# The opening of a linear-attention and gated-FFN kernel rearranged by head pairs, with two transfers and one set of transposes moved

## The chip, the cores and the metric

The kernel runs on one core of a Trainium2 chip. The metric is the device time of one execution in microseconds (us). Before the change the median of three runs is 323.31 us (322.63 to 324.01). The core has five engines with queues of their own: TensorE (PE; its weight loads are shown as PEld), VectorE (DVE), ScalarE (ACT), GpSimd (POOL) and SyncE (SP). SP and POOL also issue the transfers from and to memory.

## What is computed

Attention with cosine weights and without a softmax, on batch 8, 8 heads, 576 positions, head size 64, followed by a normalised gated feed-forward layer of width 1536:

```python
def phi(x, c, s):
    r = np.maximum(x, 0.0)
    return np.concatenate([r * c, r * s], axis=-1)     # c, s depend on the position
q_p, k_p = phi(q, cos_w, sin_w), phi(k, cos_w, sin_w)
kv  = np.einsum('bhsf,bhsd->bhfd', k_p, v)
z   = np.sum(k_p, axis=2)
num = np.einsum('bhsf,bhfd->bhsd', q_p, kv)
den = np.einsum('bhsf,bhf->bhs', q_p, z)[..., None] + 1e-06
x   = (num / den) as (4608, 512)                       # heads side by side
rms = np.sqrt(np.mean(x * x, axis=-1, keepdims=True) + 1e-06)
xn  = x / rms * rms_g
out = (silu(xn @ w_gate) * (xn @ w_val)) @ w_out
```

All inputs and the output are float32; the kernel multiplies in bfloat16.

## The kernel before, in words

The order of the work on each engine is the order of the calls in the source (`manual_schedule`, L49). An engine takes its instructions in that order. The order is written out by hand, and this is what the change edits.

**Blocks.** The rows of x are treated in blocks of 512 (four tiles of 128 rows, j = 0 to 3); block 0 is batch 0, and the last 64 positions of each batch are gathered in a block 8. For a block the steps n = 0 to 11 form gate and value for 128 columns of the hidden layer each (`half_mm`, L553, into psG and psV; silu on ScalarE; the product hT on VectorE), and the steps 12 to 15 form the output (`out_mm`, `out_store`). Work of the attention for the next batch is hung into these steps by the table `slots`: `at(block, step, where, function, ...)` enters it, `run` emits it. "pe" stands ahead of the step's products, "pre" ahead of its silu, "post" behind it.

**The attention of one batch.** `k_phi` makes kp (cosine part 0, sine part 1) from the raw k for one of nine chunks c, all four head pairs hp at once. `kvz_pe` multiplies kp by v (with a column of ones for z) into psA; `kvz_evac` copies the result to kvzs. `q_phi` and `q_tr_pe` make and transpose the q features of one tile, `q_tr_evac` copies them to qpT. `nd_pe` forms numerators and denominators of one tile in psA, `nd_post` takes the reciprocal and divides (VectorE) into xt, `x_sq` takes the mean square on ScalarE and the power on GpSimd, `x_norm` (VectorE) makes xn, `x_tr_pe` and `x_tr_evac` (or a transposing transfer) bring it to xnT.

**Batch 0** has functions of its own, since everything waits for it. z is summed by products with ones (`z0_pe`, a chunk at a time into zbank, copied to zrow by `z0_copy`, turned into columns by `z0_turn`); `kv0_pe` forms kv of one head pair from vv0, which a transfer casts on its way in; `kvz0_evac` copies both halves to kvzs. `nd0_pe` adds the 1e-6 by two small products (eps). q comes in two parts (`load_q0`), of two tiles each. `filler` issues products of zeros whose result is not read.

**Units.** The first eight steps of block 0 are cut into units (L631), so that they can begin with one tile of x: units 0 and 1 take one tile and four column blocks, units 2 and 3 two tiles and two column blocks, units 4 to 7 the other two tiles. `unit_mm` issues a unit's gate or value products, `unit_tile` those of one tile, `unit_silu` and `unit_h` the rest. L676 to L749 interleave the units with the tiles of batch 0, L913 to L923 go on with unit 5, the steps 8 to 10, `last_step` (step 11, into which the attention of batch 1 is hung) and `out_first` (the output of block 0, j-major, first the columns m of 0 to 7, then the rest; entries are run by the index of the product).

**Transfers.** SP issues k of batch 0, in two pieces by chunks, c 0 to 3 and c 4 to 8 (L149). POOL issues the rest of the opening in this order: q part 0, v in two transfers of two head pairs, q part 1, gate and value weights for n 0 to 3 and 4 to 7, k of batch 1, gate for n 8 to 11 (L211 to L229); then, among GpSimd's small operations, value for n 8 to 11, q and v of batch 1, the output weights wo in three transfers, k and v of batch 2. The raw tiles of k, q and v share a ring of five buffers.

Of the kernel before, what the change touches and what calls it, by code (L numbers as in the profile page):

```python
# [12 lines left out]
ALU = mybir.AluOpType  # L13
# [4 lines left out]
def kernel(  # L18
# [11 lines left out]
    nc = tc.nc  # L30
    B, H, S, D = q.shape
# [114 lines left out]

    g4 = one.tile([4, P], FP32, name="g4")
    nc.scalar.dma_start(out=g4[:, :], in_=moe_rms_g.rearrange("(t p) -> t p", p=P))
    for c0, c1 in ((0, 4), (4, NC)):  # L149
        nc.sync.dma_start(  # L150
            out=raw_kv("k", 0)[:, :, c0 * D : c1 * D],
            in_=kv_rows(k, 0, (0, HP))[:, :, c0 * D : c1 * D],
        )


    NTAB = 20
# [11 lines left out]
    masks.make_identity(nc, ident[:, :])  # L168
    mhalf = one.tile([P, 1], FP32, name="mhalf")
    G.memset(mhalf[:, :], -0.5)  # L170
# [3 lines left out]
    for i in range(NXT):  # L174
        G.memset(xts[i][:, DM : DM + 1], eps_col)


    wg = one.tile([P, NDT, DFF], BF16, name="wg")
# [30 lines left out]

    vv0 = one.tile([P, HP, NC * D], BF16, name="vv0")  # L210
    load_q0(0, G)  # L211
    for hp in range(0, HP, 2):
        G.dma_start(out=vv0[:, hp : hp + 2, :], in_=kv_rows(v, 0, (hp, hp + 2)))
    load_q0(1, G)
    for n in range(0, NNT - 4, 4):
        load_w(wg, moe_w_gate, n, n + 4)
        load_w(wv, moe_w_val, n, n + 4)

    eps_rows = one.tile([96, HP], BF16, name="eps_rows")
    eps_ones = one.tile([96, P], BF16, name="eps_ones")  # L220
# [5 lines left out]
        left -= part[i]  # L226
        G.memset(eps_rows[32 * i : 32 * i + 32, :], part[i] / 32)
    load_kv("k", 1, eng=G)
    load_w(wg, moe_w_gate, 8, NNT)  # L229

    def g_spread(bank, t):
        for i in range(3):
            nc.tensor.matmul(
                bank[:, t * P : (t + 1) * P], lhsT=sel[:, t, :], rhs=g3[:, i, :],
                start=(i == 0), stop=(i == 2),
            )
# [53 lines left out]
    def phi(eng, out_ap, in_ap, scale):  # L290
        if eng is A:
            A.activation(out=out_ap, in_=in_ap, func=AF.Relu, scale=scale)  # L292
# [114 lines left out]
    def z0_pe(c):  # L407
        for g in range(2):
            lo, hi = 64 * g, 64 * g + 64
            nc.tensor.matmul(  # L410
                zbank[g][:, :], lhsT=ones[lo:hi, :], rhs=kp[lo:hi, c, :, :],
                start=(c == 0), stop=(c == NC - 1),
            )

    def z0_copy(eng, g):
        copy(eng, zrow[:, g, :], zbank[g][0:1, :])
# [36 lines left out]


    def nd0_pe(j):
        for h in range(H):
            g, hp = h % 2, h // 2
            nc.tensor.matmul(
                heads[:, g, hp, :], lhsT=qpT[:, h, j * P : (j + 1) * P],
                rhs=kvzs[0][:, g, hp * E : (hp + 1) * E],  # L460
                start=(hp == 0), stop=False, skip_group_check=True,
            )
        for g in range(2):
            nc.tensor.matmul(
                heads[:, g, :, D], lhsT=eps_ones[:, :], rhs=eps_rows[:, :],
                start=False, stop=True, skip_group_check=True,
            )

    def nd_tails_pe(pair):
# [133 lines left out]
    qbank = [psV[0], psA[:, 0, :], psV[0], psV[1]]  # L603
    g_parts()
    filler(10, psC[1])
    for c in range(NC):
        k_phi(V, 0, c, 0)
        k_phi(A if c < 8 else V, 0, c, 1)
        z0_pe(c)
        if c < NDT:  # L610
            g_spread(psC[0], c)
    kv0_pe(0)
    kv0_pe(1)
    for j in range(2):
        q0_phi(V, j, 0)
        q0_phi(A, j, 1)
        q_tr_pe(0, j, qbank[j])
    z0_copy(V, 1)
# [54 lines left out]

    HALF = DM // 2  # L676
# [3 lines left out]
    q0_phi(V, 2, 0)  # L680
    q0_phi(G, 3, 0)
    q0_phi(A, 2, 1)
    q0_phi(A, 3, 1)
    filler(2, psC[1])
    nd_post(0, 0)
    q_tr_pe(0, 2, qbank[2])
    filler(1, psC[1])
    x_sq(0, 0)
    load_w(wv, moe_w_val, 8, NNT)
    nd0_pe(1)  # L690
    q0_tr_evac(V, 2, qbank[2])
    filler(2, psC[1])
    q_tr_pe(0, 3, qbank[3])
    nd_post(0, 1)
    filler(1, psC[1])
    nd0_pe(2)
    x_sq(0, 1)
    load_q(1, eng=G)
    load_kv("v", 1, eng=G)
# [7 lines left out]
    q0_tr_evac(A, 3, qbank[3])  # L707
    x_norm(0, 1)
    nd_post(0, 2)
    filler(1, psG[1])  # L710
    unit_mm(0, wg, by_rows=True)
    x_tr_pe(0, 1, psC[0])
    x_tr_evac(V, 0, 1, psC[0])
    unit_mm(0, wv)
    x_sq(0, 2)
    load_wo(0, 4)
    unit_silu(0)
    nd0_pe(3)
    nd_post(0, 3)
    x_norm(0, 2)  # L720
    unit_mm(1, wg)
    unit_mm(1, wv)
    x_sq(0, 3)
    load_wo(4, 8)
    load_wo(8, 12)
    unit_silu(1)
    x_norm(0, 3)
    unit_mm(2, wg)
    x_tr_pe(0, 2, psC[1])
    x_tr_evac(V, 0, 2, psC[1])  # L730
    unit_silu(2)
    unit_h(0)
    unit_mm(3, wg, part=(0, 6))
    x_tr_pe(0, 3, psC[0])
    x_tr_evac(A, 0, 3, psC[0])
    unit_mm(3, wg, part=(6, 8))
    unit_silu(3)
    unit_h(1)
    unit_tile(4, 2)
    unit_mm(2, wv)  # L740
    unit_h(2)
    unit_tile(4, 3)
    unit_silu(4)
    unit_mm(3, wv)
    unit_h(3)
    unit_mm(5, wg)
    unit_mm(4, wv)
    unit_silu(5)
    unit_h(4)  # L749

# [12 lines left out]
        at(0, 5 + c // 3, "post", k_phi, V, 1, c, 0)  # L763
        at(0, 5 + c // 3, "post", k_phi, A, 1, c, 1)
    for j in range(4):
        at(0, (8, 8, 9, 10)[j], "post", q_phi, V, 1, j, 0)
        at(0, (8, 9, 10, 10)[j], "post", q_phi, A, 1, j, 1)
        bank = (psC[0], psC[1], psV[0], psV[1])[j]
        if j < 2:
            at(0, 10 + j, "pe", q_tr_pe, 1, j, bank)  # L770
            at(0, 10 + j, "pre", q_tr_evac, V, 1, j, bank)
# [24 lines left out]
    def last_step():  # L796
        n = NNT - 1
        g, v = banks_of(0, n)
        run(0, n, "pe")
        half_mm(0, n, wg, g)  # L800
        kvz_pe(1)
        sg = four.tile([P, TB], FP32, name="sg", tag="sg")
        A.activation(out=sg[:, :], in_=g[:, 0:TB], func=AF.Silu)
        kvz_evac(A, 1)
        run(0, n, "pre")
# [8 lines left out]
    for j, i in ((1, 6), (2, 11), (3, 19)):  # L814
        at(0, 12, i, x_first, j)
        at(0, 12, i, x_last, j - 1)
    at(0, 12, 9, q_tr, 3, psV[0])
    at(0, 12, 21, x_norm, 1, 3)
    at(0, 12, 21, load_q, 2)
    at(0, 12, 43, x_tr, 3, psV[0])  # L820
    for nb in range(2, B):
        b = nb - 1
# [136 lines left out]
```

## Time and profile before

| | us |
|---|---|
| median of three runs (lowest, highest) | 323.31 (322.63, 324.01) |
| span of the profiled execution, first to last instruction | 321.1 |
| TensorE busy in the span | 313.6 |
| first weight product (L643) starts | 17.3 |
| gate of step 8 (L556) starts | 32.5 |
| output of block 0 (L574) starts | 42.3 |

The span is that of one execution; the runs are other executions, whose time also holds what lies around the span. Times within the span are counted from its start.

When the opening's transfers landed, each as its issue plus the time to landing that the view of transfers gives:

| transfer | issue | landed |
|---|---|---|
| k, second piece (SP) | 1.2 | 6.7 |
| q part 0 | 1.95 | 8.6 |
| v, pairs 0 and 1 | 3.0 | 9.8 |
| v, pairs 2 and 3 | 3.8 | 11.4 |
| q part 1 | 4.4 | 12.7 |
| gate, value for n 0 to 3 | 5.2, 5.9 | 15.1, 17.9 |
| gate, value for n 4 to 7 | 6.6, 7.4 | 20.4, 23.5 |
| k of batch 1 | 9.0 | 26.5 |
| gate, value for n 8 to 11 | 10.1, 16.0 | 28.9, 31.5 |
| q, v of batch 1 | 17.4, 18.4 | 34.4, 37.4 |
| wo, three transfers | 20.5, 22.3, 23.8 | 39.8, 42.3, 44.9 |

In the lists of groups and in the timeline a line names start, length, engine, source line, operation, what is written and read, shapes and count; in brackets stand the idle time of the engine ahead of it and what ended that. Operations of one engine overlap a little, so a row's length is somewhat more than the distance to the next.

### The profile page before, as it was taken

Reading aid. Unit: us, or ns where it says so; the run is one execution under the profiler, and the core shown is the slowest. Engines: PE = TensorE matmul, PEld = TensorE weight load, DVE = VectorE, ACT = ScalarE, POOL = GpSimd, SP = SyncE. Lnnn points to the kernel's source line nnn. Section 1 sums busy time; section 2 is a strip of 40 time slices with the busy share of each in tenths; the row PEclk is TensorE's granted clock in tenths of the full one; section 3 lists DMA queues with packets and bytes.
Section 4 is the critical chain, followed back from the end, with each engine's and each line's share of the span. In section 5 each row is a group of like instructions: output and inputs, shape, how many; then the busy total and the mean of one; then the engine's idle time right before and its main releaser. Section 6 shows DMA issues by size and latency. Waiting matters only on the chain.

```text
span 321.1 us, 6023 instructions
## 1 busy us (share of the span) xinstructions
PE 313.6 (98%) x2274; PEld 162.4 (51%) x2310; DVE 185.4 (58%) x382; ACT 165.8 (52%) x322; POOL 40.5 (13%) x79
## 2 busy tenths in 40 slices
PE   7999999999999999999999999999999999999996
PEld 2689564544454445444544445544544444444444
DVE  7976977668457773777457644781676034204410
ACT  5766756754574466554744575446543233223321
POOL 9771211002001100010001100100011000000000
PEclk9999999999999999999999999999999999999999
DMA  7999999788999999999799959995522500041002
GB/s 232 239 270 269 282 329 227 201 183 190 223 226 211 187 263 187 221 247 182 162 186 230 197 163 200 197 217 163 99 59 41 116 33 0 0 102 31 1 35 98
DMA packets 80092, 53.76 MB, mean 167 GB/s; under 512 B 52235, under 2 KB 74047, under 8 KB 80063
## 3 DMA queue, kind: packets, MB, share of 16 engines
q1 hardware_dynamic: 73110, 41.25, 62.1%
q0 software_dynamic: 6944, 12.13, 15.5%
q8 instruction: 18, 0.29, 0.4%
q14 instruction: 12, 0.09, 0.1%
q10 hardware_dynamic: 8, 0.00, 0.0%
HBM read 37.83 MB, written 9.44 MB: 147 GB/s over the span
## 4 chain that ended last, share of the span: by engine, by line
PE 94%; DMA 2%; DVE 1%; issue 1%; POOL 1%; ACT 0%; POOLq 0%; ACTq 0%
PE psC L574 27%; PE psV L556 27%; PE psG L556 26%; PE psV L643 2%; PE psA L449 2%; DMA vv<-in_v_dram 2%; PE psG L574 2%; PE psG L643 2%; PE psA L387 2%; PE psA L394 1%; PE psA L474 0%; PE psV L363 0%; PE psG L430 0%; PE psC L546 0%; POOL raw L135 0%
## 5 line engine op out<-in xcount | busy, mean ns | idle before, releaser
L571 DVE TENSOR_TENSOR hT<-psV,sg 128x512 bf16<-128x512 f32 x99 | 68.2, 689 | 96.5 <-PE psV L556 64.1
L556 PE MATMUL psV<-xnT,wv 128*128 128x512 bf16 x344 | 89.6, 379 | 0.7 <-issue 0.2
L570 ACT ACTIVATE sg<-psG 128x512 f32<-128x512 f32 x99 | 58.6, 592 | 60.8 <-PE psG L556 52.7
L556 PE MATMUL psG<-xnT,wg 128*128 128x512 bf16 x337 | 88.5, 379 | 0.7 <-issue 0.2
L574 PE MATMUL psC<-wo,hT 128*128 128x512 bf16 (+1 forms) x400 | 88.4, 376 | 0.4
L574 PEld LDWEIGHTS <-hT 128*128 128x128 bf16 x456 | 43.1, 98 | 47.7
L556 PEld LDWEIGHTS <-wv 128*128 128x128 bf16 x400 | 39.0, 98 | 46.8
L556 PEld LDWEIGHTS <-wg 128*128 128x128 bf16 x400 | 37.0, 98 | 39.9 <-DVE xnT L288 0.2
L520 POOL TENSOR_TENSOR rs<-ms,mhalf 128x1 f32<-128x1 f32 x36 | 20.5, 570 | 193.9 <-ACT scr L515 193.7
L286 ACT COPY osb<-psC 128x512 f32<-128x512 f32 x32 | 18.7, 585 | 49.9 <-PE psC L574 46.1
L515 ACT ACTIVATE scr<-xt 128x513 bf16<-128x513 f32 x36 | 22.8, 635 | 23.3 <-DVE xt L499 22.3
L527 DVE SCALAR_TENSOR_TENSOR xn<-xt,rs,gb 128x512 bf16<-128x512 f32 (+1 forms) x37 | 26.9, 730 | 9.9 <-POOL rs L520 9.9
L292 ACT ACTIVATE kp<-raw,tab 128x256 bf16<-128x256 f32 (+2 forms) x51 | 28.8, 607 | 2.4 <-DMA raw<-in_k_dram 2.4
L499 DVE TENSOR_TENSOR xt<-psA,rec 128x512 f32<-128x512 f32 x36 | 24.9, 691 | 1.2
L292 ACT ACTIVATE qp<-raw,tab 128x512 bf16<-128x512 f32 (+1 forms) x36 | 23.3, 666 | 1.2 <-DMA raw<-in_q_dram 1.1
L294 DVE TENSOR_SCALAR kp<-raw,tab 128x256 bf16<-128x256 f32 (+2 forms) x53 | 20.1, 428 | 0.5 <-DMA raw<-in_k_dram 0.5
L294 DVE TENSOR_SCALAR qp<-raw,tab 128x512 bf16<-128x512 f32 (+1 forms) x34 | 15.3, 463 | 4.7 <-DMA raw<-in_q_dram 4.7
L449 PEld LDWEIGHTS <-qpT 128*128 128x128 bf16 x224 | 10.6, 97 | 6.6
L556 PE MATMUL psV<-xnT_tail,wv 128*128 128x512 bf16 x48 | 12.3, 379 | 0.1
L556 PE MATMUL psG<-xnT_tail,wg 128*128 128x512 bf16 x46 | 12.0, 379 | 0.1
L288 DVE CAST vv<-raw 116x1280 bf16<-116x1280 f32 (+1 forms) x13 | 11.1, 857 | 1.3 <-DMA raw<-in_v_dram 1.3
L449 PE MATMUL psA<-kvzs,qpT 128*128 128x65 bf16 x224 | 11.4, 193 | 0.0
(102 smaller groups left out, 177.7 us busy)
## 6 DMA issues: line engine op xcount, KB each, us to landing
out_dram<-osb SPq DMA_DIRECT2D x27, 256.0 KB, 2.3
raw<-in_q_dram SPq DMA_DIRECT2D x6, 1024.0 KB, 9.1
raw<-in_k_dram SPq DMA_DIRECT2D x5, 1120.0 KB, 8.8
raw<-in_v_dram SPq DMA_DIRECT2D x5, 1120.0 KB, 9.4
raw<-in_k_dram POOLq DMA_DIRECT2D x2, 1152.0 KB, 19.2
raw<-in_v_dram POOLq DMA_DIRECT2D x2, 1152.0 KB, 15.7
out_dram<-osb SPq DMA_DIRECT2D x17, 128.0 KB, 2.6
wg<-in_moe_w_gate_dram POOLq DMA_DIRECT2D x3, 512.0 KB, 13.8
```

The costliest lines, as they stand in the source:

```text
L286: A.copy(out=o, in_=i)
L292: A.activation(out=out_ap, in_=in_ap, func=AF.Relu, scale=scale)
L294: eng.tensor_scalar(out=out_ap, in0=in_ap, scalar1=scale, scalar2=0.0, op0=ALU.mult, op1=ALU.max)
L449: nc.tensor.matmul(heads[:, g, hp, :], lhsT=qpT[:, h, j * P : (j + 1) * P], rhs=kvzs[b][:, g, hp * E : (hp + 1) * E], start=True, stop=True,)
L499: V.tensor_tensor(out=xt[:, 0:DM].rearrange("p (hp g d) -> p g hp d", g=2, d=D), in0=heads[:, :, :, 0:D], in1=rec[:, :, :].unsqueeze(3).to ...
L515: A.activation(out=scr[:, :], in_=xt[:, 0 : DM + 1], func=AF.Square, scale=1.0 / math.sqrt(DM), accum_out=ms[:, :],)
L520: G.tensor_tensor(out=rs[:, :], in0=ms[:, :], in1=mhalf[:, :], op=ALU.pow)
L527: V.scalar_tensor_tensor(out=xn_of[(b, j)][:, c], in0=x_of[(b, j)][:, c], scalar=rs_of[(b, j)][:, :], in1=gb[:, c], op0=ALU.mult, op1=ALU. ...
L556: nc.tensor.matmul(bank[:, cols[0] : cols[1]], lhsT=w[:, t, n * P : (n + 1) * P], rhs=x[:, t, cols[0] : cols[1]], start=(t == 0), stop=(t ...
L570: A.activation(out=sg[:, :], in_=g[:, 0:TB], func=AF.Silu)
L571: V.tensor_tensor(out=hT[:, n, :], in0=v[:, 0:TB], in1=sg[:, :], op=ALU.mult)
L574: nc.tensor.matmul(bank[:, 0 : cols[1] - cols[0]], lhsT=hT[:, n, j * P : (j + 1) * P], rhs=wo[:, n, cols[0] : cols[1]], start=(n == 0), st ...
```

## The change

It touches the opening, the interleaving of units and tiles, and the places of batch 1's attention in steps 7 to 12.

- k of batch 0 is loaded by head pairs, (0, 1) and (2, 3), all nine chunks in a row of 2304 bytes, in place of two pieces by chunks.
- phi of k goes by the same two halves: the cosine part on VectorE as one operation per head pair over all chunks (`k0_phi`, the table as a broadcast operand), the sine part by chunks of 128x128, five on ScalarE and four on VectorE for the lower pairs, nine on ScalarE for the upper. `z0_pe` goes by halves too.
- POOL: ident, mhalf and the small memsets go behind q part 0 or further; v of batch 0 comes as three pairs and one; q part 1 goes behind the weights for n 0 to 3; v of batch 1 goes ahead of the weights for n 8 to 11 and of q of batch 1.
- The first two tiles of q are transposed among the kv products; z's copies are both on ScalarE, the two copies of qpT on VectorE, gb on ScalarE.
- phi, transposes and copies of q's tiles 2 and 3, and nd of tile 2, go from ahead of the first unit to between the units. q's tile 3 is on VectorE in place of GpSimd. The eps products stand ahead of the others in `nd0_pe`. The units are ordered anew; unit 5's gate goes by tiles.
- Batch 1: the casts of v one to two steps earlier, `kvz_pe` at the head of step 10 in place of the middle of step 11, `q_phi` at steps 10 (tiles 0, 1) and 11 (tiles 2, 3, behind `x_sq`), all four transposes from step 11 on.

```diff
-    for c0, c1 in ((0, 4), (4, NC)):
-        nc.sync.dma_start(
-            out=raw_kv("k", 0)[:, :, c0 * D : c1 * D],
-            in_=kv_rows(k, 0, (0, HP))[:, :, c0 * D : c1 * D],
-        )
+    for hps in ((0, 2), (2, HP)):
+        load_kv("k", 0, hps)
...
     load_q0(0, G)
-    for hp in range(0, HP, 2):
-        G.dma_start(out=vv0[:, hp : hp + 2, :], in_=kv_rows(v, 0, (hp, hp + 2)))
+    masks.make_identity(nc, ident[:, :])
+    for hps in ((0, 3), (3, HP)):
+        G.dma_start(out=vv0[:, hps[0] : hps[1], :], in_=kv_rows(v, 0, hps))
+    load_w(wg, moe_w_gate, 0, 4)
+    load_w(wv, moe_w_val, 0, 4)
     load_q0(1, G)
-    for n in range(0, NNT - 4, 4):
-        load_w(wg, moe_w_gate, n, n + 4)
-        load_w(wv, moe_w_val, n, n + 4)
+    G.memset(mhalf[:, :], -0.5)
+    for i in range(NXT):
+        G.memset(xts[i][:, DM : DM + 1], eps_col)
+    load_w(wg, moe_w_gate, 4, 8)
+    load_w(wv, moe_w_val, 4, 8)
...
     load_kv("k", 1, eng=G)
-    load_w(wg, moe_w_gate, 8, NNT)
+    load_kv("v", 1, eng=G)
...
+    def k0_phi(c0, c1, part, hps):
+        o = slice(0, D) if part == 0 else slice(D, F)
+        f = NTAB if part == 0 else 0
+        for hp in range(*hps):
+            V.scalar_tensor_tensor(
+                out=kp[:, c0:c1, hp, o],
+                in0=raw_kv("k", 0)[:, hp, c0 * D : c1 * D].rearrange(
+                    "p (c d) -> p c d", d=D
+                ),
+                scalar=0.0,
+                in1=tab[:, f + c0 : f + c1].unsqueeze(2).to_broadcast([P, c1 - c0, D]),
+                op0=ALU.max, op1=ALU.mult,
+            )
...
-    for c in range(NC):
-        k_phi(V, 0, c, 0)
-        k_phi(A if c < 8 else V, 0, c, 1)
-        z0_pe(c)
+    for c in range(5):
+        k_phi(A, 0, c, 1, low)
+    k0_phi(0, NC, 0, low)
+    for c in range(5, NC):
+        k_phi(V, 0, c, 1, low)
+    for c in range(NC):
+        k_phi(A, 0, c, 1, high)
+    k0_phi(0, NC, 0, high)
+    for c in range(NC):
+        z0_pe(c, low)
         if c < NDT:
             g_spread(psC[0], c)
+    q0_phi(V, 0, 0)
+    q0_phi(A, 0, 1)
+    for c in range(NC):
+        z0_pe(c, high)
+    q_tr_pe(0, 0, qbank[0])
+    q0_phi(V, 1, 0)
+    q0_phi(A, 1, 1)
     kv0_pe(0)
-    kv0_pe(1)
...
+    q_tr_pe(0, 1, qbank[1])
     z0_copy(A, 0)
     q0_tr_evac(V, 0, qbank[0])
-    q0_tr_evac(A, 1, qbank[1])
-    V.tensor_copy(out=gb[:, :], in_=psC[0][:, :])
+    z0_copy(A, 1)
+    q0_tr_evac(V, 1, qbank[1])
+    kv0_pe(1)
+    kv0_pe(2)
     z0_turn()
-    kv0_pe(2)
     kv0_pe(3)
     kvz0_evac(A, 0)
     kvz0_evac(V, 1)
+    A.copy(out=gb[:, :], in_=psC[0][:, :])
```

The interleaving after the first norm, as it is now (from the first unit on):

```python
    unit_mm(0, wg, by_rows=True)
    x_tr_pe(0, 1, psC[0]); x_tr_evac(V, 0, 1, psC[0])
    unit_silu(0)
    unit_mm(0, wv)
    q0_phi(V, 2, 0); q0_phi(A, 2, 1)
    unit_mm(1, wg)
    q_tr_pe(0, 2, qbank[2]); q0_tr_evac(V, 2, qbank[2])
    q0_phi(A, 3, 1)
    unit_silu(1)
    q0_phi(V, 3, 0)
    unit_mm(1, wv)
    nd0_pe(2); nd_post(0, 2); x_sq(0, 2)
    load_wo(4, 8)
    q_tr_pe(0, 3, qbank[3]); q0_tr_evac(A, 3, qbank[3])
    unit_h(0)
    unit_mm(2, wg)
    nd0_pe(3); nd_post(0, 3); x_sq(0, 3)
    unit_silu(2)
    x_norm(0, 2)
    unit_mm(3, wg)
    unit_h(1)
    x_tr_pe(0, 2, psC[1]); x_tr_evac(V, 0, 2, psC[1])
    unit_silu(3)
    load_wo(8, 12)
    x_norm(0, 3)
    unit_mm(2, wv); unit_h(2)
    unit_tile(4, 2)
    unit_mm(3, wv)
    x_tr_pe(0, 3, psC[0]); x_tr_evac(A, 0, 3, psC[0])
    unit_h(3)
    unit_tile(5, 2)
    unit_tile(4, 3)
    unit_silu(4)
    unit_mm(4, wv)
    unit_tile(5, 3)
```

And batch 1:

```diff
     for j in range(4):
-        at(0, (8, 8, 9, 10)[j], "post", q_phi, V, 1, j, 0)
-        at(0, (8, 9, 10, 10)[j], "post", q_phi, A, 1, j, 1)
...
+        at(0, 10 + j // 2, "post" if j else "pre", q_phi, V, 1, j, 0)
+        at(0, 10 + j // 2, "post" if j else "pre", q_phi, A, 1, j, 1)
+    at(0, 7, "post", v_cast, G, 1, (0, 2))
     at(0, 8, "post", load_kv, "k", 2, (0, HP), G)
-    at(0, 9, "post", v_cast, G, 1, (0, 2))
-    at(0, 10, "pre", v_cast, V, 1, (2, 4))
+    at(0, 8, "post", v_cast, V, 1, (2, 4))
+    at(0, 10, "pe", kvz_pe, 1)
+    at(0, 10, "pre", kvz_evac, A, 1)
...
         half_mm(0, n, wg, g)
-        kvz_pe(1)
+        q_tr_pe(1, 0, psC[0])
+        q_tr_evac(V, 1, 0, psC[0])
...
         half_mm(0, n, wv, v)
+        q_tr(1, psC[1])
         nd_pe(1, 0)
-        q_tr(2, psV[0])
         nd_post(1, 0)
         V.tensor_tensor(out=hT[:, n, :], in0=v[:, 0:TB], in1=sg[:, :], op=ALU.mult)
         x_sq(1, 0)
         run(0, n, "post")
...
-    at(0, 12, 9, q_tr, 3, psV[0])
+    at(0, 12, 4, q_tr, 2, psV[0])
+    at(0, 12, 10, q_tr, 3, psV[0])
```

More of the change, by code (lines that the diff above doesn't have):

```diff
@@ L167 @@
     ident = one.tile([P, P], BF16, name="ident")
-    masks.make_identity(nc, ident[:, :])
     mhalf = one.tile([P, 1], FP32, name="mhalf")
-    G.memset(mhalf[:, :], -0.5)
     NXT = 4
@@ L173 @@
     eps_col = math.sqrt(DM * 1e-6)
-    for i in range(NXT):
-        G.memset(xts[i][:, DM : DM + 1], eps_col)
     wg = one.tile([P, NDT, DFF], BF16, name="wg")
@@ L405, with z0_pe @@
     heads0 = [b[:, 0 : HP * E].rearrange("p (hp e) -> p hp e", e=E) for b in psG]
-    def z0_pe(c):
+    def z0_pe(c, hps):
         for g in range(2):
@@ L410, in z0_pe @@
             nc.tensor.matmul(
-                zbank[g][:, :], lhsT=ones[lo:hi, :], rhs=kp[lo:hi, c, :, :],
+                zbank[g][:, hps[0] * F : hps[1] * F], lhsT=ones[lo:hi, :],
+                rhs=kp[lo:hi, c, hps[0] : hps[1], :],
                 start=(c == 0), stop=(c == NC - 1),
@@ L455, in nd0_pe @@
     def nd0_pe(j):
+        for g in range(2):
+            nc.tensor.matmul(
+                heads[:, g, :, D], lhsT=eps_ones[:, :], rhs=eps_rows[:, :],
+                start=True, stop=False, skip_group_check=True,
+            )
         for h in range(H):
@@ L460, in nd0_pe @@
                 rhs=kvzs[0][:, g, hp * E : (hp + 1) * E],
[L461 to L466, printed above, removed]
+                start=False, stop=(hp == HP - 1), skip_group_check=True,
             )
@@ L600, in filler @@
             )
-    qbank = [psV[0], psA[:, 0, :], psV[0], psV[1]]
+    qbank = [psV[0], psA[:, 0, :], psC[1], psC[0]]
+    low, high = (0, 2), (2, HP)
     g_parts()
     filler(10, psC[1])
+    for c in range(5):
[3 more added lines that the diff above has]
+        k_phi(V, 0, c, 1, low)
     for c in range(NC):
-        k_phi(V, 0, c, 0)
-        k_phi(A if c < 8 else V, 0, c, 1)
-        z0_pe(c)
+        k_phi(A, 0, c, 1, high)
+    k0_phi(0, NC, 0, high)
+    for c in range(NC):
+        z0_pe(c, low)
         if c < NDT:
             g_spread(psC[0], c)
-    kv0_pe(0)
-    kv0_pe(1)
[L614 to L618, printed above, removed]
+    q0_phi(V, 0, 0)
[5 more added lines that the diff above has]
+    q0_phi(A, 1, 1)
+    kv0_pe(0)
+    q_tr_pe(0, 1, qbank[1])
     z0_copy(A, 0)
     q0_tr_evac(V, 0, qbank[0])
-    q0_tr_evac(A, 1, qbank[1])
-    V.tensor_copy(out=gb[:, :], in_=psC[0][:, :])
+    z0_copy(A, 1)
+    q0_tr_evac(V, 1, qbank[1])
+    kv0_pe(1)
+    kv0_pe(2)
     z0_turn()
-    kv0_pe(2)
     kv0_pe(3)
@@ L677 @@
     lo, hi = (0, NDT // 2), (NDT // 2, NDT)
-    filler(2, psC[1])
+    load_w(wg, moe_w_gate, 8, NNT)
+    filler(1, psC[1])
     nd0_pe(0)
[L680 to L684, printed above, removed]
+    filler(4, psC[1])
     nd_post(0, 0)
-    q_tr_pe(0, 2, qbank[2])
-    filler(1, psC[1])
     x_sq(0, 0)
-    load_w(wv, moe_w_val, 8, NNT)
     nd0_pe(1)
-    q0_tr_evac(V, 2, qbank[2])
-    filler(2, psC[1])
-    q_tr_pe(0, 3, qbank[3])
+    filler(6, psC[1])
     nd_post(0, 1)
[L695 to L699, printed above, removed]
     x_norm(0, 0, (0, HALF))
     x_norm(0, 0, (HALF, DM))
+    x_sq(0, 1)
+    load_w(wv, moe_w_val, 8, NNT)
+    load_q(1, eng=G)
+    load_wo(0, 4)
     x_tr_pe(0, 0, psC[0], lo)
@@ L713 @@
     x_tr_evac(V, 0, 1, psC[0])
+    unit_silu(0)
     unit_mm(0, wv)
-    x_sq(0, 2)
-    load_wo(0, 4)
-    unit_silu(0)
+    q0_phi(V, 2, 0)
+    q0_phi(A, 2, 1)
+    unit_mm(1, wg)
+    q_tr_pe(0, 2, qbank[2])
+    q0_tr_evac(V, 2, qbank[2])
+    q0_phi(A, 3, 1)
+    unit_silu(1)
+    q0_phi(V, 3, 0)
+    unit_mm(1, wv)
+    nd0_pe(2)
+    nd_post(0, 2)
+    x_sq(0, 2)
+    load_wo(4, 8)
+    q_tr_pe(0, 3, qbank[3])
+    q0_tr_evac(A, 3, qbank[3])
+    unit_h(0)
+    unit_mm(2, wg)
     nd0_pe(3)
     nd_post(0, 3)
+    x_sq(0, 3)
+    unit_silu(2)
     x_norm(0, 2)
[L721 to L728, printed above, removed]
+    unit_mm(3, wg)
+    unit_h(1)
     x_tr_pe(0, 2, psC[1])
     x_tr_evac(V, 0, 2, psC[1])
-    unit_silu(2)
-    unit_h(0)
-    unit_mm(3, wg, part=(0, 6))
+    unit_silu(3)
+    load_wo(8, 12)
+    x_norm(0, 3)
+    unit_mm(2, wv)
+    unit_h(2)
+    unit_tile(4, 2)
+    unit_mm(3, wv)
     x_tr_pe(0, 3, psC[0])
     x_tr_evac(A, 0, 3, psC[0])
[L736 to L741, printed above, removed]
+    unit_h(3)
+    unit_tile(5, 2)
     unit_tile(4, 3)
     unit_silu(4)
-    unit_mm(3, wv)
-    unit_h(3)
-    unit_mm(5, wg)
     unit_mm(4, wv)
+    unit_tile(5, 3)
     unit_silu(5)
@@ L765 @@
     for j in range(4):
-        at(0, (8, 8, 9, 10)[j], "post", q_phi, V, 1, j, 0)
-        at(0, (8, 9, 10, 10)[j], "post", q_phi, A, 1, j, 1)
[L768 to L771, printed above, removed]
+        at(0, 10 + j // 2, "post" if j else "pre", q_phi, V, 1, j, 0)
+        at(0, 10 + j // 2, "post" if j else "pre", q_phi, A, 1, j, 1)
+    at(0, 7, "post", v_cast, G, 1, (0, 2))
     at(0, 8, "post", load_kv, "k", 2, (0, HP), G)
-    at(0, 9, "post", v_cast, G, 1, (0, 2))
-    at(0, 10, "pre", v_cast, V, 1, (2, 4))
+    at(0, 8, "post", v_cast, V, 1, (2, 4))
+    at(0, 10, "pe", kvz_pe, 1)
+    at(0, 10, "pre", kvz_evac, A, 1)
     at(0, 10, "post", load_kv, "v", 2, (0, HP), G)
@@ L800, in last_step @@
         half_mm(0, n, wg, g)
-        kvz_pe(1)
+        q_tr_pe(1, 0, psC[0])
+        q_tr_evac(V, 1, 0, psC[0])
         sg = four.tile([P, TB], FP32, name="sg", tag="sg")
         A.activation(out=sg[:, :], in_=g[:, 0:TB], func=AF.Silu)
-        kvz_evac(A, 1)
-        run(0, n, "pre")
         half_mm(0, n, wv, v)
+        q_tr(1, psC[1])
         nd_pe(1, 0)
-        q_tr(2, psV[0])
         nd_post(1, 0)
@@ L812, in last_step @@
         run(0, n, "post")
-    for j, i in ((1, 6), (2, 11), (3, 19)):
+    for j, i in ((1, 6), (2, 12), (3, 20)):
         at(0, 12, i, x_first, j)
         at(0, 12, i, x_last, j - 1)
-    at(0, 12, 9, q_tr, 3, psV[0])
-    at(0, 12, 21, x_norm, 1, 3)
-    at(0, 12, 21, load_q, 2)
+    at(0, 12, 4, q_tr, 2, psV[0])
+    at(0, 12, 10, q_tr, 3, psV[0])
+    at(0, 12, 22, x_norm, 1, 3)
+    at(0, 12, 22, load_q, 2)
     at(0, 12, 43, x_tr, 3, psV[0])
```

2 lines of the change are left out of this document (removed).

## The prediction

> **What bounds the kernel now.** I read the engine totals first, then busy time by stretch, then the chain that ended last, then the timeline of the opening and of the last step of block 0.
>
> ```profile
> PE 313.6 (98%) x2274; PEld 162.4 (51%) x2310; DVE 185.4 (58%) x382; ACT 165.8 (52%) x322; POOL 40.5 (13%) x79
> ```
> ```profile
> 15.00:17.30 2.30, 2.09 (x27) 1.37 (x26) 1.84 (x6) 1.47 (x6) 2.08 (x4) 1.00 1.24 204
> 17.30:22.00 4.70, 4.70 (x84) 4.52 (x83) 3.65 (x8) 3.12 (x7) 3.37 (x6) 1.00 1.23 229
> 22.00:27.00 5.00, 5.00 (x60) 4.63 (x58) 2.97 (x5) 2.45 (x5) 1.83 (x3) 1.00 1.14 305
> 27.00:32.00 5.00, 5.00 (x48) 4.48 (x46) 3.87 (x9) 3.74 (x9) 0.75 (x1) 1.00 1.15 288
> ```
> In the second fence each line is a stretch, its length, then busy time of PE, PEld, DVE, ACT, POOL, the granted clock, the DMA share and GB/s. From 17.3 us on TensorE has no gap. So there are two places to look: when the first weight product (L643) starts, and what is put between products afterwards. Whatever is inserted there, or makes TensorE wait there, adds one for one to the end.
>
> ```profile
> 3.02 6.81 DMA vv<-in_v_dram
> ...
> 12.56 0.43 DVE kvzs L288
> ...
> 17.46 0.90 PE psG L643 x16
> ...
> 19.60 0.24 PE psA L458 x8
> ...
> 36.08 0.45 PE psC L363 x8
> ```
> The chain (start, length, what): v's first half arrives at 9.83, the state of batch 0 is copied out (L288) at 12.56, the first product follows 4.9 us later. The last two pieces are prices: the eight products of one tile (numerator and denominator, "nd") hold TensorE 0.24 us, eight head transposes 0.45.
>
> ```profile
> 5.04 3.42 ACT L292 ACTIVATE kp<-raw,tab 128x256 bf16<-128x256 f32 x8 [2.38 <-DMA raw<-in_k_dram]
> ...
> 17.15 1.02 ACT L286 COPY qpT<-psV 128x1024 bf16<-128x1024 bf16 x1
> ...
> 19.44 0.41 PE L458 MATMUL psA<-kvzs,qpT 128*128 128x65 bf16 x8
> ...
> 19.91 0.21 DVE L487 RECIPROCAL rec<-psA 128x8 f32<-128x8 f32 x1 [0.49 <-PE psA L464]
> ...
> 20.16 0.69 DVE L499 TENSOR_TENSOR xt<-psA,rec 128x512 f32<-128x512 f32 x1
> ...
> 20.76 0.74 DVE L527 SCALAR_TENSOR_TENSOR xn<-xt,rs,gb 128x512 bf16<-128x512 f32 x1
> ...
> 20.96 0.64 ACT L515 ACTIVATE scr<-xt 128x513 bf16<-128x513 f32 x1 [0.54 <-DVE xt L499]
> ...
> 21.59 0.58 ACT L666 ACTIVATE sg<-psG 128x512 f32<-128x512 f32 x1
> ```
> This is one tile's path from its products to its norm. Products to reciprocal 0.47 (0.43 once the eps products stand first), 0.25 to the division, which holds VectorE 0.60 and ends after 0.69; 0.11 to the square; the square holds ScalarE 0.63; the copy of the transposed q on ScalarE takes 1.02.
>
> **Opening.** The same bytes are moved. v is issued about 0.2 earlier on POOL (four memsets and mhalf leave, ident now follows q's first part). k's two transfers came at 4.96 and 6.7 (issue 1.19 + 5.5) and I keep 5.0 and 6.7. ScalarE's phi of 128x128 is not in the trace: its 128x256 form repeats every 0.40 (three in 1.29, 0.50 each), the 128x512 form every 0.61 (two in 1.32), so between 0.20 and 0.40; the line through both gives 0.30. Five from 5.0, nine from 6.7: 9.4. Four q phi (1.70 in the trace): 11.1. Two zrow copies (0.56 each, 0.46 apart): 12.1. VectorE's 128x576 is nearest the norm of 128x512, which repeats every 0.67 (128x256: 0.40), so 0.74, between 0.67 and 0.85; four of them and four 128x128 (0.30; the 128x256 cost 0.26 to 0.50) end at 9.3. TensorE then sums z of the upper pairs (nine times 0.11): 10.3, transposes: 10.75, forms pair 0: 11.0, transposes after ScalarE: 11.6, forms pairs 1 and 2 (36 products in 0.54): 12.15. z's turn 0.28, pair 3 0.44 to its end: 12.85, where before the copy began at 12.54. nd gains 0.08, since VectorE's q phi no longer stands in front of its reciprocal. Net **+0.2**. Bounds: v is complete at 11.36 before (issue 3.76 + 7.6), 0.2 earlier now, so not under -1.2; at 0.40 per ScalarE phi, +1.6.
>
> **Work moved behind the first product.** Two tiles' q transposes and the nd of tile 2, which ran among filler products: 2 x 0.45 + 0.24 + 0.03 = **+1.17**. The fillers taken out stood ahead of the chain's last wait and give nothing. Units 4 and 5 have the same columns in another order: 0.
>
> **New waits among the units.** Engines take their work in program order; the changed order is printed by engine.
> (a) nd of tile 3 needs the copy of q's tile 3, which ScalarE now does behind the square of tile 2, and that needs nd of tile 2. From nd 2 on: 0.43 + 0.25 + 0.69 + 0.11 + 0.63 + 1.02 + 0.03 = 3.16. TensorE has nd 0.24, transposes 0.47, unit 2's gate 0.87, eps 0.05: 1.63. Wait **1.5** (1.2 to 1.7).
> (b) x's transposes of tile 2 need its norm, which VectorE does behind the division of tile 3: 0.43 + 0.25 + 0.60 + 0.75 + 0.03 = 2.06, against nd 0.24 and unit 3's gate 0.87. **0.95** (0.8 to 1.1).
> (c) The second tile of unit 4 reads x's tile 3, whose copy on ScalarE (0.58) follows its transposes (0.22, and 0.20 to the copy): 1.03 with 0.03, against 0.22 and one unit tile of 0.45. **0.36** (0.2 to 0.5). Before, 0.22 + 0.45 + 0.87 of products stood between.
>
> **Last step and output of block 0.** The phi of q's tiles 2 and 3 of batch 1 now goes out after the square of its tile 0; before it was done by 40.2. From nd_pe(1, 0): 1.80 to that square (41.64 to 43.44 in the timeline), 0.63 for it, 0.71 for ScalarE's phi, 0.03: 3.17. The transposes of tile 2 stand four output products later: 0.24 + 4 x 0.216 = 1.10. Wait **2.05** (1.7 to 2.2). Behind them on TensorE stand all later output products. The state of batch 1 goes to the start of step 10 with the same products; its copy on ScalarE (0.59) comes off the last step, where the chain shows 0.16 of issue: left at 0.
>
> **Queues.** POOL: a transfer there waits for an earlier one to land (wo: 0.71 behind wv at 23.80). q's second part goes behind the first two weight blocks, so it lands where the second of these did, 17.9 (5.90 + 12.0); ScalarE first wants it at 18.8 after unit 0's silu: nothing, and one for one beyond that. Gate and value of n 8 to 11 go behind v of batch 1 and land about 3.0 later (v took 34.4 to 37.4), at 31.9 and 34.4; they were read at 32.47 and 33.33 and now some 4.2 later, so the delay itself hides it. v of batch 1 lands by 30, and its casts, now two steps earlier, keep up. The powers of tiles 2 and 3 stand behind wo's issues, which wait for landings of 17.9 and 20.4; they are wanted at 23 and 26. SP keeps its two k transfers; q of batch 2 moves by one output product.
>
> **Sum.** 0.2 + 1.17 + 1.5 + 0.95 + 0.36 + 2.05 = 6.2. The profiled execution's span 321.1 becomes 327.3; it lies 2.2 under the median of the runs, 323.31, which becomes **329.5**. The bounds add up to +3.9 (-1.2 + 1.17 + 3.9) and +8.3 (1.6 + 1.17 + 5.5), so 327.2 to 331.6.
>
> **Rivals.**
> Overtaking: TensorE runs the next ready product past one that waits. Then the four waits (4.86) fill and only 0.2 + 1.17 stay: 324.7, no change. It decides if all but 0.2 us of the waits is filled. For it: a weight load of L430 was issued at 8.91, its product at 9.87. Against it: q's first transposes were ready at about 9.5 (both phi done) and stood behind products that waited for v until 9.87; they ran at 10.51, in order. 0.06. The Trainium skill ("TensorE: Matmul & The Clock Gate", Part 2, step by step) says that only weight loads are pulled ahead and products keep program order; by that rule this rival is out, and the trace agrees with 10.51 against 9.5.
> Clock: TensorE now idles from 5.0 to about 6.7 and near 8 to 9.3. If the granted clock halves, as in the first ten fillers (3.90 us for ten, 0.22 each later), about 1.7 us of products before 11.2 double, about 1.0 of it on the path: 330.5. Against it: the clock column reads 1.00 in all stretches, also over the gap of 0.57 before 9.87. 0.07. The same page, Part 1, halves the clock after an idle window of about 3.4 us; by it gaps of 1.7 and 1.3 cost nothing, and no run yet shows a gap so long here.
> Late q: its second part lands 1 us after 18.8; ScalarE holds unit 1's silu behind it: 330.5. Transfers run without a pause until 51 us, which speaks for some lateness. 0.06.
> v's arrival sets the opening (-1.2 instead of +0.2): 328.1, in the forecast's own range.
> That the change doesn't do what it says is ruled out by the printed order.
>
> **Chances.** Forecast with its bounds 0.72, overtaking 0.06, clock 0.07, late q 0.06; 0.09 for shorter waits than I priced together with an opening nearer v's arrival, half of it reaching no change, half faster. Measurement can't tell under 0.5% (1.6 us). Faster 0.05, same 0.10, slower 0.85. Range 327.2 to 331.6: it leaves out overtaking and most of the last case.
>
> **What would show it.** Right: first product near 17.5; TensorE waiting about 1.5 for a qpT copy, 0.9 for xn, 0.4 for an xnT copy between 22 and 31, and 2 us before the transposes of qp near 47; weights never waited for. Wrong: no such gaps, or a first product before 16, or a TensorE wait on a transfer.

## The result, and the profile after

The changed kernel takes 331.76 us (median of four runs: 332.96, 333.09, 329.58, 330.56) against 323.31: 2.5% slower, ratio 1.0254, 95% interval 1.0208 to 1.0301. The forecast was 329.5, and the median lies 0.16 above the end of its range, 331.6. The profiled execution is the one of 332.96; its span is 331.2, 10.1 above the 321.1 of before. Laid side by side at four marks, first start to first start:

| stretch (us) | before | after | difference | forecast |
|---|---|---|---|---|
| start to first weight product | 17.31 | 20.43 | +3.12 | +0.2 |
| from there to the gate of step 8 (units) | 15.16 | 20.18 | +5.02 | +3.98 |
| steps 8 to 11 | 9.86 | 9.42 | -0.44 | no price of its own; transposes of 0.45 cross the mark |
| output of block 0, to the first product of block 1 | 11.76 | 14.16 | +2.40 | +2.05, and those 0.45 |
| rest | 267.01 | 267.01 | 0 | 0 |

The engine totals of the changed kernel:

```profile
PE 319.1 (96%) x2303; PEld 165.0 (50%) x2339; DVE 185.8 (56%) x380; ACT 167.8 (51%) x330; POOL 37.2 (11%) x77
```

TensorE's busy time went from 313.6 to 319.1 and its idle time from 7.5 to 12.1. The busy time by stretch (start and end, length, then PE, PEld, DVE, ACT, POOL, clock, DMA share, GB/s) says where the idle time sits:

```profile
20.43:40.61 20.18, 17.17 (x225) 15.36 (x224) 14.48 (x28) 11.39 (x25) 7.77 (x11) 1.00 1.15 288
40.61:50.03 9.42, 9.31 (x129) 5.40 (x128) 5.69 (x11) 5.31 (x11) 0.00 (x0) 1.00 1.02 312
50.03:64.19 14.16, 12.27 (x96) 6.44 (x95) 10.26 (x24) 9.44 (x19) 2.20 (x4) 1.00 0.26 57
```

In the units TensorE is idle for 3.01 of 20.18 us, where before it had no gap at all; in the output of block 0 for 1.89 of 14.16 (before 0.05 of 11.76). No other engine is near its limit. The timeline (start, duration, engine, line, what; in brackets the idle time before it and what ended that) names the waits:

```profile
26.34 0.63 ACT L528 ACTIVATE scr<-xt 128x513 bf16<-128x513 f32 x1 [2.10 <-DVE xt L512]
...
26.97 0.99 ACT L284 COPY qpT<-psC 128x1024 bf16<-128x1024 bf16 x1
...
28.02 0.42 PE L476 MATMUL psA<-kvzs,qpT 128*128 128x65 bf16 x8 [1.28 <-ACT qpT L284]
...
30.13 0.40 PE L559 MATMUL psC<-ident,xn 128*128 128x128 bf16 x4 [0.81 <-DVE xn L540]
...
30.93 2.43 DVE L540 SCALAR_TENSOR_TENSOR xn<-xt,rs,gb 128x512 bf16<-128x512 f32 x1
...
31.64 1.16 POOL L286 CAST vv<-raw 128x1152 bf16<-128x1152 f32 x1
...
33.41 0.40 PE L559 MATMUL psC<-ident,xn 128*128 128x128 bf16 x4 [0.69 <-DVE xn L540]
...
34.48 0.61 PE L682 MATMUL psG<-xnT,wg 128*128 128x128 bf16 x8 [0.23 <-ACT xnT L284]
...
52.84 0.62 PE L375 MATMUL psV<-ident,qp 128*128 128x128 bf16 x8 [1.79 <-ACT qp L290]
```

Five waits of TensorE. Four are those of the forecast, on the releasers it named; the first two lines show the square of tile 2 on ScalarE (26.34) and behind it the copy (26.97) that the first wait is for. The wait at 33.41 was not forecast: the norm of tile 3 on VectorE took 2.43 us, over three times its usual 0.75, beside a cast of batch 1's v on GpSimd. A wait costs TensorE more than its idle figure, because products are pipelined and the modelled end of the last one before the gap reaches about 0.17 us past its turn. Counted from start to start, against the time the products ahead of it take in an unbroken row (0.87 for a unit's eight products of 256 columns), they cost 1.41, 0.98, 0.86, 0.39 and 1.95.

The opening is the larger surprise. In its timeline the first line is the ten fillers:

```profile
1.19 4.45 PE L611 MATMUL psC<-warm 128*128 128x512 bf16 x10 [1.19 <-DVE warm L161]
...
6.28 0.39 PE L422 MATMUL psC<-kp,ones 64*128 64x256 bf16 x1 [0.64 <-DVE kp L312]
...
11.63 0.42 PE L422 MATMUL psC<-kp,ones 64*128 64x256 bf16 x1
11.63 0.42 PE L422 MATMUL psV<-kp,ones 64*128 64x256 bf16 x1
11.84 0.42 PE L422 MATMUL psC<-kp,ones 64*128 64x256 bf16 x1
```

The pairs of z products stand 0.21 apart, twice the 0.11 that the forecast took, and still do so at 11.84. A filler of 512 columns takes 0.43, as the first seven of before do. TensorE ran at half its clock until about 13.6 us, where the first clock event of the trace stands; before, that event came at 4.4. The clock column of the views shows 1.00 ahead of the first event, so there the length of a known product has to be read instead.

### The profile page after: what moved, and what is told of

Same layout as the page of the kernel before. It is cut to its first block, busy times and chain, and to the rows that moved or that the text cites. A ratio compares the mean times of both kernels' runs of the same rounds, so it can differ in the third digit from the quotient of the medians.

```text
span 331.2 us, 6086 instructions
## 1 busy us (share of the span) xinstructions
PE 319.1 (96%) x2303; PEld 165.0 (50%) x2339; DVE 185.8 (56%) x380; ACT 167.8 (51%) x330; POOL 37.2 (11%) x77
## 4 chain that ended last, share of the span: by engine, by line
PE 92%; DVE 3%; ACT 2%; DMA 1%; issue 1%; POOL 0%; ACTq 0%
PE psC L587 26%; PE psV L569 26%; PE psG L569 26%; PE psA L462 2%; PE psA L399 2%; PE psG L587 2%; PE psV L667 1%; PE psC L422 1%; DMA raw<-in_k_dram 1%; PE psG L667 1%; DVE xn L540 1%; DVE xt L512 1%; PE psA L406 1%; ACT scr L528 1%; PE psV L375 1%
## 5 line engine op out<-in xcount | busy, mean ns | idle before, releaser
L540 DVE SCALAR_TENSOR_TENSOR xn<-xt,rs,gb 128x512 bf16<-128x512 f32 (+1 forms) x37 | 28.6, 776 | 9.0 <-POOL rs L533 9.0
L290 ACT ACTIVATE kp<-raw,tab 115x512 bf16<-115x512 f32 (+3 forms) x57 | 29.7, 569 | 2.2 <-DMA raw<-in_k_dram 2.2
L292 DVE TENSOR_SCALAR qp<-raw,tab 128x512 bf16<-128x512 f32 (+1 forms) x36 | 16.0, 460 | 4.7 <-DMA raw<-in_q_dram 4.7
L292 DVE TENSOR_SCALAR kp<-raw,tab 115x512 bf16<-115x512 f32 (+3 forms) x47 | 17.3, 415 | 0.0
```

Of the source, the lines that this page charges most:

```text
L292: eng.tensor_scalar(out=out_ap, in0=in_ap, scalar1=scale, scalar2=0.0, op0=ALU.mult, op1=ALU.max)
L540: V.scalar_tensor_tensor(out=xn_of[(b, j)][:, c], in0=x_of[(b, j)][:, c], scalar=rs_of[(b, j)][:, :], in1=gb[:, c], op0=ALU.mult, op1=ALU. ...
```

## The experiments

Each is an edit of one place, unless the text says otherwise. The ratio is to the kernel before, timed beside it on the same chip (323.25 or 323.03 there). The stretches are those of the table above, in the profiled execution.

**16 fillers in place of 10.**

```diff
-    filler(10, psC[1])
+    filler(16, psC[1])
```

> The changed kernel with 16 instead of 10 filler products in front of the sums of z. Theory: in the changed kernel's trace the full clock was granted only from 13.6 us (4.4 in the kernel before), so the products up to there took twice their time and the first weight product came at 20.4; six more filler products bring the full clock by 8.1 at the latest, the first weight product comes at 17.4 to 18.2 and the span shrinks by 2 to 3 us to about 328.5. Rival: phi of k and the copies on ScalarE and VectorE are slower than priced and set the opening; then the first product stays at 20 or later, and moves later by up to 1 us because the sums start behind the fillers.

Measured 330.21 us (329.49 to 331.44), ratio 1.022 [1.0191, 1.0248]; profiled span 327.7. TensorE in the opening of this run:

```profile
1.19 5.44 PE L611 MATMUL psC<-warm 128*128 128x512 bf16 x16 [1.19 <-DVE warm L161]
...
9.06 0.27 PE L422 MATMUL psC<-kp,ones 64*128 64x256 bf16 x1
9.06 0.27 PE L422 MATMUL psV<-kp,ones 64*128 64x256 bf16 x1
9.17 0.27 PE L422 MATMUL psC<-kp,ones 64*128 64x256 bf16 x1
...
10.14 0.62 PE L375 MATMUL psV<-ident,qp 128*128 128x128 bf16 x8
...
17.66 0.55 PE L667 MATMUL psG<-xnT,wg 128*128 128x128 bf16 x7
```

The z products stand 0.11 apart, the first transposes start at 10.14 (after: 12.41), and the first weight product at 17.66 instead of 20.43: 2.77 of the opening's 3.12 was the clock. What is left, 0.35, is the forecast's +0.2 within its bounds; up to 0.29 of it may be the fillers themselves, since the first z products came at 6.57 instead of 6.28. The full clock came at 4.91 here, when ten fillers would still have been running (all at half speed, they end at 5.64). So this execution does not show that six more bring it sooner; what they did was to fill the gap ahead of the z products, and the clock was not lost again.

The units took 19.32 instead of 20.18, though nothing in them was changed. The cast of v now stands 1 us behind the norm of tile 3, which takes 0.75 again:

```profile
28.16 0.75 DVE L540 SCALAR_TENSOR_TENSOR xn<-xt,rs,gb 128x512 bf16<-128x512 f32 x1
...
29.88 1.14 POOL L286 CAST vv<-raw 128x1152 bf16<-128x1152 f32 x1 [1.00 <-DMA raw<-in_v_dram]
```

**A late clock in the kernel before.** The same cause, put into the other kernel: five fillers in place of ten.

> The kernel before with 5 instead of 10 filler products at its start. Theory: the full clock then comes later than 4.4 us, the first weight product moves from 17.3 to between 18.5 and 20.5, and the whole run is 1 to 3 us longer: the price of a late clock by itself, without any other part of the change. Rival: the clock does not depend on those fillers, or the opening is set by v's arrival at 9.8 with enough room behind it: first product at 17.3 to 17.6, no change in time.

325.25 us (324.78 to 325.85), ratio 1.0066 [1.0041, 1.009]. The z products ran at half speed (0.42 apart, where a filler of as many columns takes 0.22 at full clock), the full clock came at 12.7, the first weight product at 19.53 instead of 17.31, and the rest of the kernel was unchanged. So a late clock alone costs this kernel 2.2 us in the profiled execution, 2.0 in the median.

**The cast of v on VectorE.**

```diff
-    at(0, 7, "post", v_cast, G, 1, (0, 2))
+    at(0, 7, "post", v_cast, V, 1, (0, 2))
```

> The changed kernel with both halves of batch 1's v cast on VectorE (steps 7 and 8); GpSimd casts nothing. Theory: the norm of tile 3 took 2.43 us instead of 0.75 since GpSimd's cast ran beside it (31.64 to 32.80); without it the norm takes 0.75 and the wait of 0.7 to 1.0 us in front of tile 3's transposes goes: minus 0.9 us between the first weight product and the gate of step 8 (20.2 us, 19.3 expected). Rival: the norm is slow for another reason (its power is late, or the transfer issues on GpSimd beside it); then it still takes 2 us or more and nothing is gained.

331.42 us (330.59 to 332.3), ratio 1.0254 [1.0221, 1.0286]. The norm of tile 3 in this run:

```profile
31.08 0.75 DVE L540 SCALAR_TENSOR_TENSOR xn<-xt,rs,gb 128x512 bf16<-128x512 f32 x1
```

It is back at 0.75, its wait is gone, the units took 19.32 (0.86 less), and steps 8 to 11 lost nothing by the cast (9.41). The runs hardly show it, since the opening, which was late here too (20.58), varies by more from run to run.

**The phi of q's tiles 2 and 3 of batch 1 at step 10.**

```diff
-        at(0, 10 + j // 2, "post" if j else "pre", q_phi, V, 1, j, 0)
-        at(0, 10 + j // 2, "post" if j else "pre", q_phi, A, 1, j, 1)
+        at(0, 10, "post" if j else "pre", q_phi, V, 1, j, 0)
+        at(0, 10, "post" if j else "pre", q_phi, A, 1, j, 1)
```

> The changed kernel with phi of q's tiles 2 and 3 of batch 1 issued at step 10 instead of behind the square of tile 0 in step 11. Theory: the wait of 1.8 to 2.3 us in front of the transposes of tile 2 goes, and nothing takes its place: minus 2 us from the first output product to the first product of block 1 (14.3 us in the changed kernel, 12.3 expected). Rival: ScalarE is then late with the silu of steps 10 and 11 and the wait only moves there: minus 0.5 us at most over steps 10, 11 and the output together.

330.63 us (328.15 to 331.4), ratio 1.0216 [1.0172, 1.0259]. The wait of 1.79 is gone, and the output of block 0 took 12.45 instead of 14.16; steps 8 to 11 took 9.61 instead of 9.42. So 1.7 of the stretch's 1.95 came from the place of that phi behind the square, and 0.2 went back into steps 8 to 11: less than the forecast 2, since a little of it did move. This profile also shows the clock as a column (third figure from the right), by stretch:

```profile
4.48:7.88 3.40, 2.24 (x20) 0.97 (x18) 3.37 (x10) 3.17 (x11) 3.40 (x10) 1.00 1.05 274
7.89:11.29 3.40, 3.40 (x33) 2.22 (x31) 1.75 (x5) 2.73 (x8) 1.67 (x7) 0.50 1.18 194
...
24.96:28.36 3.40, 1.59 (x21) 1.14 (x18) 1.72 (x4) 1.84 (x4) 1.31 (x2) 1.00 1.05 352
28.37:31.77 3.40, 3.13 (x21) 2.62 (x22) 2.59 (x5) 1.36 (x4) 2.92 (x4) 0.50 1.24 214
```

Here the full clock came at 4.47, as in the kernel before, and was lost from 7.89 to 11.30: the stretch ahead of it holds the gap of the opening (2.24 busy of 3.40). It was lost again from 28.37 to 31.78, behind a stretch that holds the wait of 1.28 and most of that of 0.81 (1.59 busy). The second loss shows in the units, which took 20.82 instead of 19.32 (the norm of tile 3 took 0.74 in this run).

**The copy of q's tile 3 ahead of the square of tile 2.**

```diff
-    x_sq(0, 2)
-    load_wo(4, 8)
     q_tr_pe(0, 3, qbank[3])
     q0_tr_evac(A, 3, qbank[3])
+    x_sq(0, 2)
+    load_wo(4, 8)
```

> The changed kernel with the head transposes of q's tile 3 and ScalarE's copy of them ahead of the square of tile 2, instead of behind it. Theory (nd of tile 3 waits 1.28 us because that copy stands behind the square): TensorE's wait for a qpT copy goes, the wait for the norm of tile 2 stays near 0.8, and the stretch from the first product to the gate of step 8 is 18.9 us instead of 20.18 where the clock comes as late as in the changed kernel's profile; the run 1.2 to 1.3 us shorter at equal opening. Rival (the copy is late for another reason, or the square that is now behind it makes the norm of tile 2 later by the copy's 1.0 us): the wait only moves to the norm of tile 2, which grows from 0.8 to about 1.8, and the stretch stays within 0.4 us of 20.2.

329.53 us (329.51 to 330.94), ratio 1.0214 [1.0196, 1.0232]. TensorE's waits in the units of this run:

```profile
25.47 0.42 PE L476 MATMUL psA<-kvzs,qpT 128*128 128x65 bf16 x8 [0.20 <-ACT qpT L284]
27.57 0.40 PE L559 MATMUL psC<-ident,xn 128*128 128x128 bf16 x4 [0.81 <-DVE xn L540]
31.06 0.61 PE L682 MATMUL psG<-xnT,wg 128*128 128x128 bf16 x8 [0.23 <-ACT xnT L284]
```

The wait for the copy fell from 1.28 to 0.20, and the next one did not grow. The units took 18.24: 1.08 below the 19.32 of the runs with a norm of 0.75, which this one has too. The size is 0.2 short of the forecast 1.3, since the copy then waits for its transposes.

**All four remedies together.** The four edits above, in one kernel.

> The changed kernel with all four remedies: 16 fillers in the opening, q's tile 3 copied ahead of the square of tile 2, the cast of batch 1's v (pairs 0 and 1) on VectorE, and the phi of q's tiles 2 and 3 of batch 1 at step 10. Theory (a late clock, ordinary waits and the cast beside the norm are separate and add): first product at 17.7, from there to step 8's gate 20.18 - 1.28 - 0.86 = 18.0, output products to block 1 12.4; first product of block 1 near 57.5, span 324.5, run near 326.5, ratio 1.010. What stays against the kernel before is 1.17 of work moved behind the first product, 0.8 + 0.2 of waits and 0.35 of opening. Rival (the waits are one queue: take one away and the next takes its place): units stay above 19 us, run above 328.5, ratio above 1.016.

327.39 us (326.99 to 328.21), ratio 1.014 [1.0126, 1.0155]. Units 18.24 (forecast 18.0), output of block 0 12.45 (12.4): the waits add, and none took another's place. The median was 0.9 above the forecast. In the profiled execution, the longest of the four, the span was 1.9 above its forecast of 324.5, and 0.9 of that was the opening: the full clock came at 6.9, the 16 fillers took 6.41 us, the first z products had to wait for them until 7.53, and the first weight product came at 18.63 instead of 17.7. The rest was 0.2 in the units, 0.2 in steps 8 to 11 and 0.5 behind the first product of block 1. A filler row long enough for a late clock is too long for the data.

**The norm of tile 2 ahead of the division of tile 3.** As the last one, with x_norm(0, 2) moved up between nd0_pe(3) and nd_post(0, 3).

> As the run with all four remedies, and VectorE does the norm of tile 2 ahead of the division of tile 3. Theory (the norm of tile 2 waits for nothing but its place behind that division): the wait for xn before the transposes of tile 2 falls from 0.8 to below 0.4, the stretch from the first product to step 8 is 0.4 to 0.8 us shorter than in that run, the run likewise (near 325.9). Rival (the square of tile 2, now behind ScalarE's copy, is as late): no difference, within 0.2 us.

328.14 us (327.87 to 328.71), ratio 1.0162 [1.0149, 1.0176]: a miss, neither the gain of the theory nor the standstill of the rival. The units took 19.23, 1.0 more than without the move. In VectorE's and TensorE's timeline:

```profile
26.22 0.75 DVE L540 SCALAR_TENSOR_TENSOR xn<-xt,rs,gb 128x512 bf16<-128x512 f32 x1 [1.36 <-POOL rs L533]
26.88 0.20 DVE L500 RECIPROCAL rec<-psA 128x8 f32<-128x8 f32 x1
27.03 0.40 PE L559 MATMUL psC<-ident,xn 128*128 128x128 bf16 x4 [0.77 <-DVE xn L540]
...
29.18 0.61 PE L682 MATMUL psG<-xnT,wg 128*128 128x128 bf16 x8 [0.89 <-ACT sg L690]
```

VectorE now waits 1.36 for the power of tile 2's square on GpSimd, and the norm starts only 0.06 sooner than behind the division, counted from the first weight product (26.22 - 18.46 = 7.76, against 26.45 - 18.63 = 7.82 in the run before). The wait for it stays (0.77), and the division and square of tile 3, now behind it, delay unit 2's silu on ScalarE, for which unit 4's products wait 0.89.

**Work added to the kernel before.** The transposes of q's tiles 2 and 3 done once more, right behind the first weight product.

```diff
     unit_mm(0, wg, by_rows=True)
+    q_tr_pe(0, 2, psC[1])
+    q_tr_pe(0, 3, psC[1])
     x_tr_pe(0, 1, psC[0])
```

> The kernel before with 16 head transposes done twice: q's tiles 2 and 3 are transposed once more right behind the first product, into a free bank that nobody reads. Theory (TensorE has no gap there, so whatever is put behind the first product lengthens the run one for one): 2 x 0.45 = 0.90 us more between the first product and the gate of step 8 (16.06 instead of 15.16), run 324.2, ratio 1.0028. Rival (TensorE's work there hides other latencies, so that added work is partly absorbed): below 0.3 us more, ratio within 1.001.

323.70 us (323.27 to 323.98), ratio 1.0018 [1.0009, 1.0027]. The units took 15.93 instead of 15.16: 0.77 of the 0.90, and the median rose by 0.67. Work put behind the first product there costs most of its own time. The opening, unchanged here, shows another arrival of the full clock, 5.81, without a loss.

No kernel here beats the one before: with all remedies the changed one still carries the moved work, what is left of the waits and a later opening.

## Why the prediction came out as it did

- **Direction and place.** Right: the loss lies in the opening, the units and the output of block 0, and nowhere else. Without the clock (2.77) and the slow norm (0.86) the span would be 327.6, against a forecast of 327.3; the run with 16 fillers, which had neither, took 327.7.
- **Waits among the units** (forecast 1.5, 0.95 and 0.36; 2.81). Measured, start to start, 1.41, 0.98 and 0.39; 2.78. The first is shown by its removal: the copy on ScalarE stood behind the square. The second agrees with its forecast cause in the timeline: the power of tile 2 ended at 27.71, and its norm started at 29.32, right behind the division of tile 3. Lifting the norm was tried only where the copy already stands ahead of the square; there the power is nearly as late as the division, and nothing is gained. The third was not tried.
- **Moved work** (1.17). Measured in the rows of TensorE 1.35: two sets of transposes 0.45 and 0.49, the small eps products 0.06 and nd of tile 2 0.35 (forecast 0.03 and 0.24).
- **Last step** (2.05). Measured 1.95; 1.7 of it went when the phi was done earlier.
- **Queues.** Right in what was priced at nothing: q's second part landed at 18.0 (forecast 17.9), v of batch 1 at 29.96 (by 30), and TensorE waited for no transfer in the units. But "v of batch 1 lands by 30, and its casts, now two steps earlier, keep up" looked at the cast's own time only. It did not ask what VectorE does meanwhile; that was the norm of tile 3, and it cost 0.86 in this execution. In the profiles where the cast fell at another time, the units were that much shorter, but for the one that lost its clock there. The meeting also hangs on the late opening: with a timely clock the norm ran at 28.16 and the cast waited for v until 29.88, while here the norm had moved to 30.93 and the cast stood at 31.64. The Trainium skill ("SBUF — State Buffer", Who interferes with whom) says that a VectorE instruction with two SBUF inputs contends with a GpSimd instruction that reads SBUF, and that the order of issue decides which of them blocks. The norm has two such inputs, and 0.75 against 2.43 agrees; by the rows the norm started first (30.93 against 31.64) and yet it was the one drawn out, so the order is not shown, GpSimd's spans being rough.
- **Opening, the step that failed** (+0.2, measured +3.12). The chain of phi and products itself was right: 17.66 with a timely clock, against 17.5. The term at fault was the clock: the sum had it at nothing, and it stood as a rival with chance 0.07 and "about 1.0 of it on the path". It held in this execution, and it cost 2.8. Two readings were wrong. The forecast took the full clock at 4.4 for given (TensorE "idles from 5.0"), while ten fillers at half speed are 4.4 us of products, to 5.64. The z products of before start at 5.66, so that even such a row reaches them; in the changed kernel they come at 6.28, behind a gap. In two of four profiles with this opening the full clock came only at 13.6 and 14.0; in the other two it came at 4.5 and 4.8, was lost from about 8 to 11.5, and the first product stood at 18.9. And the forecast argued from a rule that an idle stretch of 3.4 us is needed.

The Trainium skill ("TensorE: Matmul & The Clock Gate", Part 1, What's actually happening) says that the clock is set by windows of 3413 ns that run freely and do not start with the kernel. With that the changes 3.41 apart agree (4.47, 7.89, 11.30; 28.37, 31.78), and so does the luck of the opening. But the halving does not need an idle window: stretches with 2.24 and 1.59 of 3.40 busy were enough. That the gap ahead of the z products makes the clock late agrees with five fillers in the kernel before (a gap of 2.17, full clock at 12.7) and with the three profiles with 16 fillers (no gap, full clock at 4.9, 6.5 and 6.9).

The slow norm had a sign in the trace of before, between the two casts of batch 1's v:

```profile
37.45 1.15 POOL L288 CAST vv<-raw 128x1152 bf16<-128x1152 f32 x1 [9.66 <-DMA raw<-in_v_dram]
37.79 1.42 DVE L288 CAST vv<-raw 128x1152 bf16<-128x1152 f32 x1
```

VectorE's cast took 1.42 beside GpSimd's there, and 0.74 in the run with added work, where it came after it. It cost TensorE nothing, so none of its waits shows it; the length of the row does.

The parts add up: 2.77 clock, 0.35 opening, 1.35 moved work, 2.78 and 0.86 waits in the units, 1.95 in the output, 10.06 of the 10.1. The median is 8.45 above that of before, since two of the four runs were shorter than the profiled one, with spans of 327.8 and 328.8. A first product at 18.95, as in the run with the copy moved, and a norm of 0.75 would give 331.2 - 1.48 - 0.86 = 328.9. The granted clock of the run with 328.8, 0.994, fits that: the run with the copy moved has 0.995 with one stretch of 3.41 us at half speed. The one with 327.8 (0.999) is as short as the run with 16 fillers and its timely clock (327.7). Neither of the two has a profile, so this is an inference.

## What to carry to other kernels

Price a moved call by what stands ahead of it on its own engine when its consumer wants it: four such sums came out within 0.1 us here. Where a change opens a gap in TensorE's first microseconds, treat the clock as a price of its own (2 to 3 us here) and read it from the length of a known product. When an instruction moves to another time on GpSimd, look at what VectorE does then.

## What the runs showed of the hardware

The clock was halved again behind stretches in which TensorE was busy 2.24 of 3.40 us (many products of 64 and of four rows) and 1.59 of 3.40 us. It stayed full behind others that were no busier than the first: counted on in steps of 3.41 us from its first clock event, the changed kernel's profile has 1.83 of 3.41 busy from 27.26 to 30.67 and 1.67 from 51.15 to 54.56. In that profile it also stayed at half over a stretch from 6.8 to 10.2 us in which products followed each other without a gap, many of them of four rows. So the busy share alone does not decide; whether rows count, and from what share on the clock falls, was not tried.

A GpSimd cast of 1.16 us drew a VectorE instruction of 0.75 us out to 2.43, more than both one after the other (1.91). In the profile with the early phi a cast began, by the rows, 0.2 us before the end of such a norm; the norm took 0.74 and the cast 1.22 instead of 1.14.
